# Two ways for each up product of an expert, for 384 or for 512 rows

## The chip, the cores and the metric

One core of one Trainium2 chip runs the whole program. The metric is the time of one execution on the device in microseconds (us). Three timed runs of the kernel before gave 1068.37, 1067.69 and 1065.72 us; their median is 1067.69 us.

## The reference: what is computed

Three stages follow one another, all in float32, on 3072 tokens of width 512.

```python
# 1  linear attention with decay, 4 sequences x 8 heads x 768 steps x 64
state = gamma * state + outer(k_t, v_t);  y_t = scale * q_t @ state
# 2  a dense gated layer, 512 -> 1536 -> 512
x = ((x @ w_a) * (x @ w_b)) @ w_out
# 3  eight experts, each token goes to the one with its largest logit
e_idx = argmax(x @ w_gate)                       # 3072 tokens, 8 experts
for e in range(8):
    h  = maximum(x[e_idx == e] @ w1[e], 0)       # up:   512 -> 1024
    ye = h @ w2[e]                               # down: 1024 -> 512
    out[e_idx == e] = gate_w * eom * ye
```

How many tokens an expert gets is known only on the chip, after the logits. The mean is 384.

## The kernel before, in words

The change lies in the third stage. `BASE, CAP = 384, 512` (L33): every expert is computed for 384 gathered rows, and a fourth tile of 128 rows only where the expert has more than 384 tokens. `n_e` is the count of an expert, held in a register of every engine. What is above 512 rows goes to a loop at the end (`overflow`, L676).

Matmuls are made in float32 precision out of three: `mm3` (L104 to 107) multiplies high and low halves of both operands, so each product of a 128x128 weight tile costs three matmuls, one per line. `up(p, f, d, c0, n)` (L626) makes the up product of feature tile `f` (there are `NF2` = 8 of 128 features) for `n` rows from `c0`: 4 weight tiles x 3 = 12 matmuls into one PSUM bank. `up2` (L632) does so into bank `ph[f % 2]`. `relu` (L639) turns that bank into the pair of halves `hs[f]`: one ScalarE instruction for the high half (L636), one VectorE instruction for the low half (L637). `down2` (L644) multiplies `hs[f]` with the second weight matrix, three matmuls of 512 columns for each tile of 128 rows, and adds them up in the banks `accs[t]` over all `f`. `finish` (L651) scales a finished bank and sends it to the output by an indirect DMA of POOL. While an expert runs, the weights of the next one are loaded by the SP queue (`load_raw`, L421) and split into halves (`split_part`, L668, ScalarE and VectorE), its rows are gathered by POOL (`gather`, L607) and turned by TensorE (`turn`, L615).

`expert` (L695 to 754) writes out the order by hand; every engine issues its instructions in the order of the program text. For each `f` TensorE makes `up2(f)` for 384 rows, then what `rest(f)` holds, then `down2(f - 1)`. `rest` (L707) is the part under a condition: `with tc.If(n_e > BASE)` (L714) makes the up product of the fourth tile (12 matmuls of 128 columns into the bank `px`), its relu (`hx`), and the down product of the fourth tile one step behind (three matmuls into `accs[3]`). It is called for `f` = 0 to 8, so an expert has nine such blocks; expert 0 has none, since it always has 512 rows, 256 of them done ahead. There is no `Else`. All five engines branch at each block, whether they have work in it or not. An engine that skips a block adds to its semaphore what the block would have added, so that later waits hold on either way; that addition waits until the engine's own earlier work is counted. At the end of an expert `up2(0)` of the next one is issued (L754), for 384 rows.

Of the kernel before, what the change touches and what calls it, by code (L numbers as in the profile page):

```python
# [7 lines left out]
F32 = mybir.dt.float32  # L8
F32R = mybir.dt.float32r
# [10 lines left out]
E, FF2 = 8, 1024  # L20
# [8 lines left out]
NF2 = FF2 // 128  # L29
# [3 lines left out]
BASE, CAP = 384, 512  # L33
LEAD = 256
# [19 lines left out]
def attention_moe_moe2(ctx: ExitStack, tc: tile.TileContext, a: dict, out: bass.AP):  # L54
# [4 lines left out]
    p2 = ctx.enter_context(tc.tile_pool(name="p2", bufs=2))  # L59
    ps1 = ctx.enter_context(tc.tile_pool(name="ps1", bufs=1, space=bass.MemoryType.PSUM))  # L60
    psg = ctx.enter_context(tc.tile_pool(name="psg", bufs=2, space=bass.MemoryType.PSUM))
# [6 lines left out]
    def lp(n):  # L68
        if not late:
            for _ in narrowing:  # L70
                pass
            early.close()
            for k in (1, 2, 3, 5):
                late[k] = ctx.enter_context(tc.tile_pool(name=f"l{k}", bufs=k))
        return late[n]
# [7 lines left out]
    arena = cpool.tile([128, NF1, 2, 2, 512], F32R, name="arena")  # L83
# [16 lines left out]
    idx = cpool.tile([128, E, 4, 4], I32, name="idx")  # L100
# [3 lines left out]
    def mm3(outp, wh, wl, rh, rl, start, stop):  # L104
        pe.matmul(outp, lhsT=wh, rhs=rh, start=start, stop=False)  # L105
        pe.matmul(outp, lhsT=wh, rhs=rl, start=False, stop=False)  # L106
        pe.matmul(outp, lhsT=wl, rhs=rh, start=False, stop=stop)  # L107

    def f32(ap):
        return ap.bitcast(F32)  # L110
# [310 lines left out]
    def load_raw(key, src):  # L421
        t = lp(2).tile([128, 2, 512], F32, tag="wraw", name="wraw")
        sync.dma_start(t, src)
        rawq[key] = t
# [121 lines left out]
    accs = {}  # L546
# [40 lines left out]
    def load_idx0(j0):  # L587
        rows = tab_d[LEAD * (j0 // 2) : LEAD * (j0 // 2) + LEAD, :]
        sync.dma_start(idx[:, 0, j0 : j0 + 2], rows.rearrange("(j p) c -> p j c", j=2))
# [17 lines left out]
    def gather(e, jt, rows=T):  # L607
        fetch(idx[:, e, jt], (e, jt), rows)
# [3 lines left out]
    def xst(e):  # L612
        return turned if e % 2 else xs

    def turn(key, d, c0):  # L615
        t = gath.pop(key)
        pt = psg.tile([128, 4, 128], F32, tag="gen", name="pg")
        for k in range(KD):
            pe.transpose(pt[:, k], t[:, 128 * k : 128 * k + 128], ident)
        s = slice(c0, c0 + 128)  # L620
        act.copy(d[:, 0, :, s], pt)
        dve.tensor_tensor(d[:, 1, :, s], pt, f32(d[:, 0, :, s]), op=ALU.subtract)

    ph = {}

    def up(p, f, d, c0, n):  # L626
        cc = slice(c0, c0 + n)
        for k in range(KD):
            kk = slice(128 * k, 128 * k + 128)
            mm3(p[:, :n], arena[:, f, 0, 0, kk], arena[:, f, 0, 1, kk], d[:, 0, k, cc], d[:, 1, k, cc], k == 0, k == KD - 1)  # L630

    def up2(f, d, c0, n, which=None):  # L632
        up(ph[f % 2 if which is None else which], f, d, c0, n)

    def relu_to(h, p, n):
        act.activation(h[:, 0, :n], p[:, :n], AF.Relu)  # L636
        dve.scalar_tensor_tensor(h[:, 1, :n], p[:, :n], 0.0, f32(h[:, 0, :n]), op0=ALU.max, op1=ALU.subtract)  # L637

    def relu(f, n, which=None):  # L639
        h = p2.tile([128, 2, 512], F32R, tag="gs", name="hs")  # L640
        relu_to(h, ph[f % 2 if which is None else which], n)
        return h

    def down2(f, h, rows, a0=0, t0=0):  # L644
        for t, m in enumerate(rows, t0):
            if f == 0:
                accs[t] = ps1.tile([128, 512], F32, tag=f"acc{a0 + t}", name=f"acc{a0 + t}")
            tt = slice(128 * t, 128 * t + m)
            mm3(accs[t][:m], h[:, 0, tt], h[:, 1, tt], arena[:, f, 1, 0], arena[:, f, 1, 1], f == 0, f == NF2 - 1)

    def finish(ix, t, y, m=128):  # L651
        y, ix, acc = y[:m, t], ix[:m], accs[t][:m]
        if t % 2:
            dve.tensor_scalar(y, acc, ix[:, 2:3].bitcast(F32), None, op0=ALU.mult)
        else:
            act.activation(y, acc, AF.Copy, scale=ix[:, 2:3].bitcast(F32))  # L656
        st = pool.indirect_dma_start(  # L657
            out=out[:, :],
            out_offset=bass.IndirectOffsetOnAxis(ap=ix[:, 1:2], axis=0),
            in_=y,  # L660
            in_offset=None,
            bounds_check=T - 1,
            oob_is_err=False,
        )
        tc.declare_no_dep(st.ins, group="rows", reason="each token's row is in one slot")
        tc.add_to_no_dep_group("rows", st.ins)

    def split_part(key, f, part):  # L668
        t = rawq[key] if part == 0 else rawq.pop(key)
        act.copy(arena[:, f, part, 0], t[:, part])  # L670
        dve.tensor_tensor(arena[:, f, part, 1], t[:, part], f32(arena[:, f, part, 0]), op=ALU.subtract)  # L671

    def ytile():
        return p1.tile([128, 4, 512], F32, tag="xraw", name="y")
# [17 lines left out]
                        down2(f, relu(f, 128, 1), [128])  # L692
                    finish(it, 0, ytile())

    def expert(e, j0, n, n_e=None):  # L695


        rows = [min(128, n - t) for t in range(0, n, 128)]
        d = xst(e)
        nx = e + 1  # L700
        more = nx < E
        hs, hx = {}, {}
        y = ytile()
        if n_e is not None:
            accs[3] = ps1.tile([128, 512], F32, tag="acc3", name="acc3")

        def rest(f):  # L707

            if n_e is None:
                return  # L710
            px = psg.tile([128, 512], F32, tag="gen", name="px") if f < NF2 else None
            if f < NF2:
                hx[f] = lp(2).tile([128, 2, 128], F32R, tag="hx", name="hx")
            with tc.If(n_e > BASE):  # L714
                if f < NF2:
                    up(px, f, d, BASE, CAP - BASE)
                    relu_to(hx[f], px, CAP - BASE)
                if f > 0:
                    h = hx.pop(f - 1)
                    mm3(accs[3], h[:, 0], h[:, 1], arena[:, f - 1, 1, 0], arena[:, f - 1, 1, 1], f == 1, f == NF2)  # L720
                if f == NF2:
                    finish(idx[:, e, 3], 3, y)

        if more:
            load_raw(("ex", nx, 0), a["ex"][nx, 0])
            load_raw(("ex", nx, 1), a["ex"][nx, 1])
        hs[0] = relu(0, n)
        rest(0)
        for f in range(1, NF2 + 1):
            if f < NF2:  # L730
                up2(f, d, 0, n)
                hs[f] = relu(f, n)
            rest(f)
            if more:
                split_part(("ex", nx, f - 1), f - 1, 0)
            if more and f <= 4:
                gather(nx, f - 1)
            if more or f < NF2 - 1:
                down2(f - 1, hs.pop(f - 1), rows)
            if more and f < NF2:  # L740
                split_part(("ex", nx, f - 1), f - 1, 1)
                if f + 1 < NF2:
                    load_raw(("ex", nx, f + 1), a["ex"][nx, f + 1])
            if more and 3 <= f <= 6:
                turn((nx, f - 3), xst(nx), 128 * (f - 3))
        if not more:
            tc.mark_branch_hint_location("over", "LikelyTaken")
        for t, m in enumerate(rows):
            for f in hs:
                down2(f, hs[f], [m], 0, t)  # L750
            finish(idx[:, e, j0 + t], t, y, m)
        if more:
            split_part(("ex", nx, NF2 - 1), NF2 - 1, 1)
            up2(0, xst(nx), 0, BASE)  # L754


    with tc.manual_schedule():
# [45 lines left out]
        for j, blk in enumerate(BLOCKS):  # L803
            n = 256 * len(blk)
            ntile = n // 128
            last = j == len(BLOCKS) - 1
            att = attention_steps(j + 1) if not last else []
            if last:
                first = lambda: (load_idx0(0), gather(0, 0, T - 256), gather(0, 1, T - 256))
# [69 lines left out]
        hs = {}  # L879
# [8 lines left out]
        n_e = []  # L888
# [17 lines left out]
        y = ytile()  # L906
        for t in range(2):
            finish(idx[:, 0, t], t, y)
        up2(0, xs, 0, LEAD)

        expert(0, 2, CAP - LEAD)
        for e in range(1, E):
            expert(e, 0, BASE, n_e[e])
        with tc.If(n_e[E] > CAP, preferred_fallthrough_block=True, label="over"):
            overflow()

# [69 lines left out]
```

## Time and profile before

| | |
|---|---|
| median of three runs | 1067.69 us |
| the profiled execution, its own time | 1067.26 us |
| its span, from the first to the last instruction | 1065.0 us |
| TensorE matmuls, busy | 1028.6 us (97%) |
| VectorE, ScalarE, POOL, busy | 615.7, 390.2, 278.6 us |
| mean granted TensorE clock | 0.986 of full speed |

The profile is of one execution. PE is TensorE's matmuls, PEld its weight loads, DVE is VectorE, ACT is ScalarE, SP issues most DMAs. The letter q behind an engine (PEldq, ACTq) means its sequencer, which handles branches and semaphores. Matmuls are pipelined: the duration of one contains its latency, and the distance between two starts is what one costs in a row of them. In the timeline a line has the start and the duration in us, the engine, the line of the kernel, the operation, output and inputs, the shape, and in brackets how long the engine sat idle before it and what ended that.

### The profile page before, as it was taken

The numbers are of one execution on the slowest core, as the hardware profiler recorded it, in microseconds if no ns is written. First come the engines' busy times: TensorE is split into PE (matmuls) and PEld (weight loads), VectorE is DVE, ScalarE is ACT, GpSimd is POOL, SyncE is SP. The second block draws the span as 40 slices with busy tenths as digits, with TensorE's granted clock in tenths as the row PEclk, the third lists the DMA queues.
The fourth block names the chain that finished last, engine by engine and source line by source line (L and its number), as shares of the span: only waits on it lengthen the run. The fifth ranks groups of instructions, "written<-read, shape, count | busy, mean of one in ns | idle before, by whom it ended". The sixth has DMA issues, their size and how long they took to land. (4 is left out here: it accounts for less than half of the span.)

```text
span 1065.0 us, 20296 instructions
## 1 busy us (share of the span) xinstructions
PE 1028.6 (97%) x7893; PEld 862.4 (81%) x7894; DVE 615.7 (58%) x1399; ACT 390.2 (37%) x791; POOL 278.6 (26%) x241
## 2 busy tenths in 40 slices
PE   6899999999999999999999999999999999999997
PEld 4687778888888788878888889898888899988876
DVE  5798887665675567655765763643644444445431
ACT  3466662223222332223222334442544433334331
POOL 1456442113121411231124243423202203030211
PEclk7799999999999999999999999999999999999999
DMA  8666645222532243224222423523644424243410
GB/s 319 215 220 226 204 151 171 90 80 62 179 118 80 60 149 124 96 61 158 80 67 63 159 71 110 149 90 94 224 137 167 167 79 158 91 160 122 164 65 27
DMA packets 51674, 138.61 MB, mean 130 GB/s; under 512 B 10973, under 2 KB 11229, under 8 KB 51552
## 3 DMA queue, kind: packets, MB, share of 16 engines
q1 hardware_dynamic: 43920, 117.16, 33.0%
q0 software_dynamic: 6928, 19.46, 5.8%
q8 instruction: 69, 1.13, 0.4%
q10 hardware_dynamic: 720, 0.57, 0.2%
q14 instruction: 37, 0.30, 0.1%
HBM read 121.37 MB, written 16.96 MB: 130 GB/s over the span
## 5 line engine op out<-in xcount | busy, mean ns | idle before, releaser
L105 PE MATMUL p<-xs,arena 128*128 128x512 f32 (+1 forms) x672 | 249.2, 371 | 8.1 <-DVE z L220 4.3
L107 PE MATMUL p<-xs,arena 128*128 128x512 f32 (+1 forms) x672 | 243.3, 362 | 0.6 <-POOL arena L458 0.6
L106 PE MATMUL p<-xs,arena 128*128 128x512 f32 (+1 forms) x672 | 243.1, 362 | 0.0
L515 POOL TENSOR_TENSOR wos<-wo,wos 128x512 fp32r<-128x512 f32 x72 | 99.3, 1380 | 281.2 <-ACT wos L514 275.9
L105 PEld LDWEIGHTS p<-xs,arena 128*128 128x128 f32 x672 | 127.7, 190 | 31.4 <-issue 9.1
L107 PEld LDWEIGHTS p<-xs,arena 128*128 128x128 f32 x672 | 127.7, 190 | 20.8 <-POOL arena L458 1.0
L106 PEld LDWEIGHTS p<-xs,arena 128*128 128x128 f32 x672 | 127.9, 190 | 18.9
L542 ACT CAST gs<-g_sb 128x512 fp32r<-128x512 f32 (+1 forms) x84 | 47.0, 559 | 213.5 <-DVE g_sb L540 213.5
L340 DVE SCALAR_TENSOR_TENSOR junkd<-x,wcol 128x512 bf16<-128x512 f32 x144 | 121.9, 847 | 3.6
L671 DVE TENSOR_TENSOR arena<-wraw,arena 128x512 fp32r<-128x512 f32 x112 | 77.5, 692 | 78.8 <-ACT arena L670 77.5
L105 PE MATMUL acc<-wos,gs 128*128 128x512 f32 x288 | 115.0, 399 | 0.0
L107 PE MATMUL acc<-wos,gs 128*128 128x512 f32 x288 | 113.2, 393 | 0.0
L106 PE MATMUL acc<-wos,gs 128*128 128x512 f32 x288 | 112.4, 390 | 0.0
L637 DVE SCALAR_TENSOR_TENSOR hs<-ph,hs 128x384 fp32r<-128x384 f32 (+1 forms) x72 | 38.0, 527 | 103.6 <-ACTq L714 64.9
L540 DVE TENSOR_TENSOR g_sb<-p,a_sb 128x512 f32<-128x512 f32 (+1 forms) x84 | 51.3, 610 | 79.2 <-PE p L107 70.0
L657 POOL DMA_INDIRECT out<-y,idx x27 | 27.7, 1025 | 263.1 <-ACT y L656 173.2
L670 ACT CAST arena<-wraw 128x512 fp32r<-128x512 f32 x112 | 68.7, 619 | 71.1 <-PE acc L107 65.6
L105 PE MATMUL acc<-arena,hs 128*128 128x512 f32 x200 | 82.6, 413 | 6.9 <-PEq L714 1.4
L543 DVE TENSOR_TENSOR gs<-g_sb,gs 128x512 fp32r<-128x512 f32 (+1 forms) x84 | 52.1, 621 | 52.5 <-ACT gs L542 52.5
L106 PE MATMUL acc<-arena,hs 128*128 128x512 f32 x200 | 79.1, 396 | 0.0
L107 PE MATMUL acc<-arena,hs 128*128 128x512 f32 x200 | 78.9, 394 | 0.0
L636 ACT ACTIVATE hs<-ph 128x384 fp32r<-128x384 f32 (+1 forms) x72 | 33.6, 467 | 117.1 <-PE ph L107 115.6
(167 smaller groups left out, 1803.5 us busy)
## 6 DMA issues: line engine op xcount, KB each, us to landing
wraw<-in_ex SPq DMA_DIRECT2D x64, 512.0 KB, 3.3
wo<-wo_d SPq DMA_DIRECT2D x72, 256.0 KB, 2.6
wide<-in_w_ab SPq DMA_DIRECT2D x24, 512.0 KB, 4.0
qk<-in_qk SPq DMA_DIRECT2D x23, 512.0 KB, 4.3
vk<-in_vk SPq DMA_DIRECT2D x23, 512.0 KB, 5.4
wcol<-in_wgt SPq DMA_DIRECT2D x20, 512.0 KB, 5.1
wide<-in_w_out SPq DMA_DIRECT2D x12, 512.0 KB, 4.2
x_d<-x SPq DMA_DIRECT2D x24, 256.0 KB, 2.1
```

The lines of the kernel that those rows point to most:

```text
L105: pe.matmul(outp, lhsT=wh, rhs=rh, start=start, stop=False)
L106: pe.matmul(outp, lhsT=wh, rhs=rl, start=False, stop=False)
L107: pe.matmul(outp, lhsT=wl, rhs=rh, start=False, stop=stop)
L340: dve.scalar_tensor_tensor(junk, x2t[i], 1.0, wc[:, e], op0=ALU.mult, op1=ALU.mult, accum_out=st["lg"][:, e0 + e : e0 + e + 1])
L515: pool.tensor_tensor(w[:, 1], t, f32(w[:, 0]), op=ALU.subtract)
L540: dve.tensor_tensor(g[:, :n], pb[:, :n], ta[:, :n], op=ALU.mult)
L542: act.copy(gs[:, 0, :n], g[:, :n])
L543: dve.tensor_tensor(gs[:, 1, :n], g[:, :n], f32(gs[:, 0, :n]), op=ALU.subtract)
L636: act.activation(h[:, 0, :n], p[:, :n], AF.Relu)
L637: dve.scalar_tensor_tensor(h[:, 1, :n], p[:, :n], 0.0, f32(h[:, 0, :n]), op0=ALU.max, op1=ALU.subtract)
L670: act.copy(arena[:, f, part, 0], t[:, part])
L671: dve.tensor_tensor(arena[:, f, part, 1], t[:, part], f32(arena[:, f, part, 0]), op=ALU.subtract)
```

## The change

The part under a condition is no longer a block beside the up product: the up product itself has two ways. `first(f)` opens the condition before `up2(f)`. Where the expert has more than 384 tokens it makes the three down matmuls of the fourth tile of the step before (`rest(f - 1)`), then `up2(f)` for 512 rows and one relu for 512; in the `Else` it makes `up2(f)` and the relu for 384 rows. `px` and `hx` are gone, the fourth tile is part of `hs[f]`. `last` does the same for the end: `rest(7)`, the down product of `f` = 7 and the output of the fourth tile in one way, the down product alone in the other. For the last expert only the first tile's products of `f` = 6 and 7 are in the two ways, the other tiles follow behind. The `up2(0)` that is issued for the next expert has two ways as well, by that expert's count (`after`). Expert 0 stays without a condition but for that last product.

```diff
-    def expert(e, j0, n, n_e=None):
+    def expert(e, j0, n, n_e, after):
...
-        hs, hx = {}, {}
+        hs = {}
...
         def rest(f):
-            if n_e is None:
-                return
-            px = psg.tile([128, 512], F32, tag="gen", name="px") if f < NF2 else None
-            if f < NF2:
-                hx[f] = lp(2).tile([128, 2, 128], F32R, tag="hx", name="hx")
-            with tc.If(n_e > BASE):
-                if f < NF2:
-                    up(px, f, d, BASE, CAP - BASE)
-                    relu_to(hx[f], px, CAP - BASE)
-                if f > 0:
-                    h = hx.pop(f - 1)
-                    mm3(accs[3], h[:, 0], h[:, 1], arena[:, f - 1, 1, 0], arena[:, f - 1, 1, 1], f == 1, f == NF2)
-                if f == NF2:
-                    finish(idx[:, e, 3], 3, y)
+            mm3(accs[3], hs[f][:, 0, BASE:], hs[f][:, 1, BASE:], arena[:, f, 1, 0], arena[:, f, 1, 1], f == 0, f == NF2 - 1)
+
+        def first(f):
+            hs[f] = p2.tile([128, 2, 512], F32R, tag="gs", name="hs")
+            if n_e is None:
+                if f:
+                    up2(f, d, 0, n)
+                return relu_to(hs[f], ph[f % 2], n)
+            with tc.If(n_e > BASE) as some:
+                if f:
+                    rest(f - 1)
+                    up2(f, d, 0, CAP)
+                relu_to(hs[f], ph[f % 2], CAP)
+            with some.Else():
+                if f:
+                    up2(f, d, 0, BASE)
+                relu_to(hs[f], ph[f % 2], BASE)
+
+        def seconds(some_rows, t0):
+            for f in (NF2 - 1,) if more else (NF2 - 2, NF2 - 1):
+                down2(f, hs[f], some_rows, 0, t0)
+
+        def last():
+            own = rows if more else rows[:1]
+            with tc.If(n_e > BASE) as some:
+                rest(NF2 - 1)
+                seconds(own, 0)
+                finish(idx[:, e, 3], 3, y)
+            with some.Else():
+                seconds(own, 0)
...
-        hs[0] = relu(0, n)
-        rest(0)
+        first(0)
         for f in range(1, NF2 + 1):
             if f < NF2:
-                up2(f, d, 0, n)
-                hs[f] = relu(f, n)
-            rest(f)
+                first(f)
...
-            if more or f < NF2 - 1:
+            if f == NF2 and n_e is not None:
+                last()
+            elif more or f < NF2 - 1:
                 down2(f - 1, hs.pop(f - 1), rows)
...
         for t, m in enumerate(rows):
-            for f in hs:
-                down2(f, hs[f], [m], 0, t)
+            if t and not more:
+                seconds([m], t)
             finish(idx[:, e, j0 + t], t, y, m)
         if more:
             split_part(("ex", nx, NF2 - 1), NF2 - 1, 1)
-            up2(0, xst(nx), 0, BASE)
+            with tc.If(after > BASE) as some:
+                up2(0, xst(nx), 0, CAP)
+            with some.Else():
+                up2(0, xst(nx), 0, BASE)
...
-        expert(0, 2, CAP - LEAD)
-        for e in range(1, E):
-            expert(e, 0, BASE, n_e[e])
+        for e in range(E):
+            expert(e, 0 if e else 2, BASE if e else CAP - LEAD, n_e[e] if e else None, n_e[e + 1])
```

## Rows read from the trace of the kernel before

**Rows 1.** The page's first part: busy time, share of the span, instructions.

```profile
PE 1028.6 (97%) x7893; PEld 862.4 (81%) x7894; DVE 615.7 (58%) x1399; ACT 390.2 (37%) x791; POOL 278.6 (26%) x241
```

**Rows 2.** Windows by expert (1, 3, 4): length, busy per engine, granted clock, DMA.

```profile
762.96:801.98 39.02, 37.67 (x186) 31.59 (x185) 19.59 (x32) 17.44 (x31) 6.57 (x7) 1.00 0.45 147
...
840.93:892.64 51.71, 51.71 (x306) 47.14 (x305) 21.45 (x39) 18.51 (x38) 7.02 (x8) 1.00 0.35 118
892.64:944.36 51.72, 51.72 (x305) 47.14 (x304) 21.49 (x40) 18.50 (x38) 8.03 (x9) 1.00 0.35 120
```

**Rows 3.** Tile px: count, ns min/median/max, first and last start.

```profile
L105 PE MATMUL px<-arena x32: 221/274/276, 843.0 to 886.7; 128*128 128x128 f32 x32
...
L105 PE MATMUL px<-xs,arena x32: 220/274/276, 894.7 to 938.4; 128*128 128x128 f32 x32
```

**Rows 4.** Timeline of TensorE in expert 3: where each run of matmuls begins.

```profile
848.49 0.40 PE L105 MATMUL acc<-arena,hs 128*128 128x512 f32 x1
...
850.59 0.33 PE L105 MATMUL ph<-arena 128*128 128x384 f32 x1
...
852.69 0.22 PE L105 MATMUL px<-arena 128*128 128x128 f32 x1
...
853.98 0.46 PE L105 MATMUL acc<-arena,hx 128*128 128x512 f32 x1
...
856.84 0.33 PE L105 MATMUL ph<-arena 128*128 128x384 f32 x1
```

**Rows 5.** Timeline of TensorE in the dense layer, twelve matmuls of 512 columns apart.

```profile
500.84 0.39 PE L105 MATMUL p<-xs,arena 128*128 128x512 f32 x1
...
503.59 0.39 PE L105 MATMUL p<-xs,arena 128*128 128x512 f32 x1
```

**Rows 6.** Timeline of TensorE around a skipped block of expert 1.

```profile
767.60 0.34 PE L107 MATMUL ph<-arena 128*128 128x384 f32 x1
...
768.09 0.47 PE L105 MATMUL acc<-arena,hs 128*128 128x512 f32 x1
...
768.39 0.39 PE L106 MATMUL acc<-arena,hs 128*128 128x512 f32 x1
...
768.62 0.39 PE L107 MATMUL acc<-arena,hs 128*128 128x512 f32 x1
```

**Rows 7.** Line L714 by sequencer: whole span, then 765.0 to 768.2, then 840.0 to 843.0.

```profile
L714 PEldq COMPARE_BRANCH  x81: 70/208/414, 761.8 to 1054.5; - x81
...
L714 PEldq EVENT_SEMAPHORE  x45: 51/51/51, 765.5 to 1054.8; - x45
...
L714 PEldq EVENT_SEMAPHORE  x2: 51/51/51, 765.5 to 768.0; - x2
...
L714 PEldq COMPARE_BRANCH  x1: 169/169/169, 842.0 to 842.0; - x1
```

**Rows 8.** Waits of the weight loads, 762 to 1061: total us, times, longest.

```profile
PEld acc L105 <- issue: 17.2, 38, 0.6
PEld ph L105 <- issue: 2.2, 5, 0.4
```

**Rows 9.** Timeline in expert 3: a relu at its start, then one of f = 1.

```profile
843.21 0.49 ACT L636 ACTIVATE hs<-ph 128x384 fp32r<-128x384 f32 x1 [0.89 <-PE ph L107]
...
846.27 0.33 PE L107 MATMUL ph<-arena 128*128 128x384 f32 x1
...
846.64 0.49 ACT L636 ACTIVATE hs<-ph 128x384 fp32r<-128x384 f32 x1 [1.82 <-PE ph L107]
...
847.16 0.56 DVE L637 SCALAR_TENSOR_TENSOR hs<-ph,hs 128x384 fp32r<-128x384 f32 x1 [2.02 <-ACT hs L636]
```

**Rows 10.** Groups by line and shape: instructions of 512 columns that read PSUM.

```profile
L535 ACT COPY a_sb<-p 128x512 f32<-128x512 f32 x60 | 35.0, 584 | 78.7 <-PE p L107 75.9 <-PE rp L319 2.8
...
L656 ACT ACTIVATE y<-acc,idx 128x512 f32<-128x512 f32 x16 | 11.0, 688 | 8.7 <-PE acc L107 8.6
...
L622 DVE TENSOR_TENSOR arena<-pg,arena 128x512 fp32r<-128x512 f32 x16 | 10.9, 683 | 0.0
```

## The prediction

> **What bounds the kernel now.** I read the page's first part, then windows by expert, then the tile that the change removes, then the timeline of TensorE, and last the line of the condition and the waits. The chain of waits says nothing here: it ends after one piece, the last output DMA. The first part says that TensorE is busy for 97% of the span, no other engine for more than 58% [rows 1]. So a change counts by what it takes from or adds to TensorE's row of matmuls, and by the holes in that row.
>
> The windows show two kinds of expert. Expert 1 takes 39.02 us, experts 3 and 4 take 51.71 and 51.72 us, at full granted clock in all three [rows 2]. The reader is to see that in the long ones the busy time of TensorE equals the window, while expert 1 has holes. The tile px says which experts enter the block: 32 matmuls of each line (4 weight tiles x 8 features) in one stretch from 843.0 and 32 in one from 894.7 [rows 3]. So only two of the seven experts with a condition have more than 384 tokens in this input, and five skip the block, nine times each. That agrees with the 45 semaphore additions on TensorE's sequencer [rows 7].
>
> **What a block costs where it is entered.** In expert 3 one whole step runs from 850.59 to 856.84: 6.25 us [rows 4]. Of it the up product for 384 rows takes 852.69 - 850.59 = 2.10, px 853.98 - 852.69 = 1.29, and twelve down matmuls (three of the fourth tile, nine of the others) 856.84 - 853.98 = 2.86. Nine down matmuls alone take 850.59 - 848.49 = 2.10, that is 0.233 each, so the fourth tile's three cost 0.76. A matmul of 384 columns costs 0.175, one of 128 columns 1.29 / 12 = 0.108: a third of the columns, over half of the time.
>
> **What a block costs where it is skipped.** Matmuls of 384 columns start 0.175 apart, but the last one before a skipped block and the first one behind it are 768.09 - 767.60 = 0.49 apart, and the next step is 0.30 in place of 0.233 [rows 6]: 0.32 + 0.07 = 0.39 us lost. The cause is not the branch: the one at 842.0 is handled 1.2 us before ScalarE gets the finished product at 843.21 [rows 7, 9], so TensorE's sequencer runs ahead. It is the semaphore addition, which stands at 768.0, when the last matmul (767.60 + 0.34) has just ended: it waits until TensorE has drained. The weight loads show the same holes, 38 in front of a down product and 5 in front of an up product [rows 8]; the 5 are the block of f = 0, one for each skipping expert. Check: by these prices an entering expert has 8 x (1.29 + 0.76) = 16.4 us of extra work and a skipping one 9 x 0.39 = 3.5 us of holes, 12.9 apart; the windows are 51.71 - 39.02 = 12.7 apart.
>
> **The change, part by part.**
>
> *The wide product, in the two entering experts.* Twelve matmuls of 384 and twelve of 128 become twelve of 512. The trace has this shape in the dense layer: twelve apart are 503.59 - 500.84 = 2.75 [rows 5]; at the pace of the down product it would be 12 x 0.233 = 2.80. A step then costs 2.75 to 2.80 for up and 12 x 0.233 = 2.80 for down, 5.55 to 5.60 in place of 6.25: 0.65 to 0.70 less. The step f = 0 has no down product: 2.10 + 1.29 = 3.39 becomes 2.75 to 2.80, 0.59 to 0.64 less. Per expert 7 x 0.68 + 0.62 = 5.4, for both 10.8 (10.3 to 11.1). TensorE is the bound in these windows, so this counts in full.
>
> *ScalarE and VectorE.* One relu of 512 in place of one of 384 and one of 128. Nothing waits on their total: in expert 3 they are busy for 18.5 and 21.5 of 51.7 us [rows 2]. I cost it at nothing; the cover is TensorE's row. Only the delay to the first reader counts, which is the next part.
>
> *rest(f - 1) moved to the head of the way.* It needs hs[f - 1]. From the last up matmul's start to ScalarE's start are 846.64 - 846.27 = 0.37, to be 0.43 with a matmul of 512; the high half then takes 0.58 to 0.69 (nearest rows of 512 columns out of PSUM), VectorE follows 0.03 after its end and takes 0.68 [rows 9, 10]. High half ready 1.0 to 1.1 after that start, low half 1.7 to 1.8. For f of 2 to 8 nine down matmuls stand between: rest would start 0.23 + 2.10 = 2.33 after it, its low half is read two matmuls later. 1.2 and 1.0 us to spare: no cost. For f = 1 nothing stands between, since up2(0) ends the expert before. TensorE then waits 1.1 - 0.23 = 0.87 for the high half, 0.2 more for the low half and loses 0.07 in the restart: I take 1.2 per entering expert (0 if the trace's order hid it, 1.8 if ScalarE came later; it sat idle for 0.89 before the relu at 843.21 [rows 9], so it comes in time). Two experts: +2.4.
>
> *The two ways and their joins.* A join must leave each semaphore at one value. TensorE counts 15 matmuls in the long way and 12 in the short one, so the short way has 3 to add, while ScalarE and VectorE count the same in both. No row of before shows a condition with an `Else`. Between nothing (the last matmul counts for them) and 0.39 per join (as in rows 6, with the addition at the end of the short way), I take 0.39, because the addition in the skipped block is exactly this case. Both ways are equal for TensorE at f = 0 (no matmuls) and at the new two-way up2(0). So a skipping expert pays 8 times (f = 1 to 7 and the end) and no longer 9: 5 x 0.39 = 2.0 less. The long way has nothing to add. Like ends keep the readers behind the join on the same count, which by these rows costs and saves no time.
>
> *Added branches.* 63 blocks become 70, on five sequencers. TensorE's branch takes 208 ns in the median [rows 7], but ahead of the work; after a join its sequencer has nine down matmuls, 2.1 us, to get ahead again. I cost it at nothing; without that cover it would be 0.2 x 70 = 14 us.
>
> The row says that a jump over the skipped block ends well ahead of the matmuls, and that no wait of a weight load for issue in this stage is over 0.6 us [rows 7, 8]. The Trainium skill, Runtime: NRT & Kernel Launch, section Instruction fetch mechanics, says that a taken branch whose target is not in the loaded window has to wait for a fetch of the target page. That speaks against the change, since now the entering experts jump too, over the `Else`; by the rows the jumps of this length have not paid it, and the sum goes by the rows. If they paid, it would be the second rival.
>
> **The sum.** -10.8 + 2.4 - 2.0 = -10.4 us. The profiled execution took 1067.26, which gives 1056.9; it lies 0.4 below the median of 1067.69, so I predict 1057 us. Its own range, from the bounds above: 1054 to 1060.
>
> **Rivals.**
> 1. *The joins cost nothing.* If the last matmul of the short way carries the three missing counts, the 40 waits that I keep vanish as well: 40 x 0.39 = 15.6 more, 1041.7 us. For it: both ways end in the same kind of instruction, so there is one to carry them. Against: the only additions in the trace are separate and wait for the drain. 25%.
> 2. *The long way pays at its end.* The entering experts had no hole at all; if the jump over the `Else` or its join costs them a hole, it is 9 places (f = 1 to 7, the end, up2(0)) x 2 x 0.39 = 7.0: 1064 us. Against: they jump today without one. 8%.
> 3. *Slower: rest at the head waits at every step.* If ScalarE or VectorE is held up behind a split of the next weights by more than the 1.0 us to spare, each of f = 2 to 8 costs the 1.2 us of f = 1: 7 x 2 x 1.2 = 16.8, so 1057 + 16.8 = 1074 us. It decides from about 2.3 us between the last up matmul and the high half. Against: the relu at 846.64 starts 0.04 after the product's end, in the middle of an entering expert [rows 9]. 8%.
>
> That the change doesn't do what it says would mean that the same two experts don't take the long way; the counts come from the same registers as before, so this has, with all else, 7%.
>
> **How the numbers follow.** Forecast 52%, rivals 25, 8 and 8%, the rest 7%. A measurement here can tell about 0.3%, 3.2 us. Faster by more than that: forecast, first rival, about half of the second and a little of the rest, 0.83. Within 0.3%: the other half of the second and about half of the rest, 0.08. Slower: the third and what is left, 0.09. The range of 1040 to 1064 takes in the first two cases and most of the second rival; outside are the third and the rest.
>
> **What would show it.** px gone, and 192 matmuls into ph of 512 columns, 0.23 apart. Windows of about 47.5 us for experts 3 and 4 (51.7 - 5.4 + 1.2) and 38.6 for a skipping one. 40 semaphore additions on TensorE's sequencer, each with a hole of 0.49 from start to start; none, and windows near 35.5, would be rival 1. One hole of about 1.1 us at f = 1 of experts 3 and 4, in front of the down product of the fourth tile; seven more in each would be rival 3. Holes at the end of the long way would be rival 2. The prediction is wrong if the windows of skipping experts move by more than 1 us, or those of the entering ones by less than 3.

## The result and the profile after

The changed kernel takes 1041.86 us (median of 4 runs, 1040.78 to 1043.57), the kernel before beside it 1067.68: ratio 0.9763, 95% interval 0.9744 to 0.9781, or 25.8 us less. The forecast was 10.7 us less. The time is that of the first rival, 1041.7. It lies outside the range that the prediction worked out from its bounds (1054 to 1060) and inside its wide one (1040 to 1064). The span fell from 1065.0 to 1040.1 us, at a granted clock of 0.986 in both.

The page's first part after the change answers to [rows 1]: TensorE stays the bound, with 192 matmuls and 20.0 us of busy time fewer.

```profile
PE 1008.6 (97%) x7701; PEld 845.2 (81%) x7702; DVE 610.4 (59%) x1383; ACT 383.9 (37%) x775; POOL 278.9 (27%) x241
```

The windows by expert of the changed kernel, experts 1 to 4 (columns as in [rows 2], to which they answer):

```profile
763.85:799.24 35.39, 35.39 (x186) 31.91 (x185) 18.86 (x31) 16.60 (x31) 6.81 (x6) 1.00 0.49 162
799.24:834.62 35.38, 35.38 (x186) 31.90 (x185) 18.24 (x30) 16.09 (x30) 6.88 (x7) 1.00 0.51 170
834.62:881.93 47.31, 46.57 (x210) 37.46 (x208) 19.74 (x32) 17.05 (x30) 6.88 (x7) 1.00 0.38 129
881.93:929.19 47.26, 46.52 (x209) 37.47 (x208) 19.59 (x32) 17.05 (x30) 8.24 (x8) 1.00 0.39 132
```

The entering experts 3 and 4 take 47.3 us (forecast 47.5). The skipping ones take 35.4 where 38.6 was forecast, and in them TensorE's busy time now equals the window (they moved by 3.6 us, and more than 1 us was the prediction's own sign of being wrong), while expert 1 had 1.35 us of idle time and several stretched starts before [rows 2, 6]. By the starts of the windows the 24.9 us of span are: experts 1 and 2 3.6 each, experts 3 and 4 4.4 and 4.5, the three skipping ones at the end with the output 9.7 (expert 5 began at 944.36 before and begins at 929.19), less 0.9 by which expert 1 began later in this execution. The forecast had 10.4 for the whole.

The timeline of TensorE in expert 1 of the changed kernel, at the place where [rows 6] had a hole:

```profile
767.86 0.34 PE L107 MATMUL ph<-arena 128*128 128x384 f32 x1
768.04 0.39 PE L105 MATMUL acc<-arena,hs 128*128 128x512 f32 x1
768.26 0.40 PE L106 MATMUL acc<-arena,hs 128*128 128x512 f32 x1
```

The last up matmul and the first down matmul start 0.18 us apart (0.49 before), the next step takes 0.22 (0.30 before). The join costs TensorE nothing. The sequencers' view of the three conditions (the product, the end, `up2(0)`) says why, beside [rows 7]:

```profile
L718 PEldq COMPARE_BRANCH  x72: 73/202/337, 762.5 to 1023.6; - x72
...
L735 PEldq COMPARE_BRANCH  x9: 73/202/212, 793.5 to 1025.9; - x9
...
L735 POOLq INC_SWDGE_SEM  x5: 470/610/665, 769.8 to 1003.3; - x5
L735 DVEq EVENT_SEMAPHORE  x5: 21/21/21, 799.3 to 1030.7; - x5
...
L771 PEldq COMPARE_BRANCH  x9: 70/202/320, 762.2 to 997.2; - x9
```

TensorE's branches are there, 90 in place of 81. Its 45 separate additions are gone. What is left is one addition of VectorE and one of POOL for the end of each skipping expert, where the short way has no instruction of theirs. The reading is that the last matmul of the `Else` also adds what the three missing ones would have added. The profile doesn't hold the amounts, so this is inferred, and the experiments test it.

The waits of the weight loads after the change, from 762 to the end (answers to [rows 8], whose 43 waits for issue are gone):

```profile
PEld acc L105 <- ACT hs L636: 2.7, 3, 1.2
PEld acc L107 <- DVE hs L637: 0.9, 2, 0.4
PEld acc L107 <- DVEq L735: 0.3, 1, 0.3
```

The largest is the wait at f = 1. The timeline of the changed kernel in expert 3 shows it:

```profile
837.13 0.39 PE L107 MATMUL ph<-arena 128*128 128x512 f32 x1
...
837.61 0.60 ACT L636 ACTIVATE hs<-ph 128x512 fp32r<-128x512 f32 x1 [1.60 <-issue]
838.23 0.69 DVE L637 SCALAR_TENSOR_TENSOR hs<-ph,hs 128x512 fp32r<-128x512 f32 x1 [1.47 <-ACT hs L636]
...
838.25 0.50 PE L105 MATMUL acc<-arena,hs 128*128 128x512 f32 x1 [0.74 <-ACT hs L636]
...
838.59 0.40 PE L106 MATMUL acc<-arena,hs 128*128 128x512 f32 x1
...
838.98 0.50 PE L107 MATMUL acc<-arena,hs 128*128 128x512 f32 x1
...
839.32 0.40 PE L105 MATMUL ph<-arena 128*128 128x512 f32 x1
```

From the last up matmul to the next product are 839.32 - 837.13 = 2.19 us. Four starts in a row would be 4 x 0.23 = 0.92, so the wait costs 1.27 (forecast 1.2). The product in two lengths, in the same expert:

```profile
842.07 0.39 PE L105 MATMUL acc<-arena,hs 128*128 128x512 f32 x1
...
844.86 0.39 PE L105 MATMUL ph<-arena 128*128 128x512 f32 x1
...
847.59 0.39 PE L105 MATMUL acc<-arena,hs 128*128 128x512 f32 x1
```

Down 2.79, up 2.73, the step 5.52 us (forecast 5.55 to 5.60; 6.25 before).

### The profile page after: what moved, and what is told of

Its sections match the earlier page's. It is cut to its first block, busy times and chain, and to the rows that moved or that the text cites. A ratio compares the mean times of both kernels' runs of the same rounds, so it can differ in the third digit from the quotient of the medians.

```text
span 1040.1 us, 19789 instructions
## 1 busy us (share of the span) xinstructions
PE 1008.6 (97%) x7701; PEld 845.2 (81%) x7702; DVE 610.4 (59%) x1383; ACT 383.9 (37%) x775; POOL 278.9 (27%) x241
## 5 line engine op out<-in xcount | busy, mean ns | idle before, releaser
L637 DVE SCALAR_TENSOR_TENSOR hs<-ph,hs 128x384 fp32r<-128x384 f32 (+2 forms) x72 | 40.1, 558 | 121.9 <-ACT hs L636 108.9
L671 DVE TENSOR_TENSOR arena<-wraw,arena 128x512 fp32r<-128x512 f32 x112 | 76.5, 692 | 48.4 <-ACT arena L670 38.6
L105 PE MATMUL acc<-arena,hs 128*128 128x512 f32 x216 | 86.7, 402 | 2.1 <-ACT hs L636 1.5
L107 PE MATMUL acc<-arena,hs 128*128 128x512 f32 x216 | 85.8, 397 | 0.0
L106 PE MATMUL acc<-arena,hs 128*128 128x512 f32 x216 | 85.4, 395 | 0.0
L636 ACT ACTIVATE hs<-ph 128x384 fp32r<-128x384 f32 (+2 forms) x72 | 35.4, 491 | 134.4 <-PE ph L107 88.9
```

## The experiments

All ratios are to the kernel before on the same chip, with the 95% interval. The theory: what saved the 15.6 us is that the short way holds an instruction of TensorE, which carries the missing counts. The rivals: where the branch stands, the `Else` as such, or the like ends.

**The changed kernel again (a1)**, as the measure for e1, e2 and e4, which ran on the same chip. e5, e6 and e9 ran on another, where the kernel before took 1071.87 in place of 1069.67 us, so their spans compare with a1's only to some 2 us; the ratios take this out.

> The changed kernel as it is, on the chip of the next three, as their measure. Theory (the last matmul of the short way carries the three missing counts, so all 45 holes of before are gone): -10.8 for the wide product, +2.4 for the wait at f = 1, -17.6 for 45 holes of 0.39: ratio 0.976. Rival (the holes went because the branch now stands ahead of the up product and is hidden): the same number here; the next runs tell them apart.

Measured: 1040.68 us, 0.9736 [0.9722, 0.9751], span 1040.3.

**One matmul of 8 columns in the skipped way of the kernel before (e1).** Into `px`, read by nobody.

```diff
-            px = psg.tile([128, 512], F32, tag="gen", name="px") if f < NF2 else None
+            px = psg.tile([128, 512], F32, tag="gen", name="px")
...
-            with tc.If(n_e > BASE):
+            with tc.If(n_e > BASE) as some:
...
+            with some.Else():
+                pe.matmul(px[:, :8], lhsT=tri[:, 0], rhs=gap, start=True, stop=True)
```

> The kernel before, with an Else of one matmul of 8 columns in each conditional block; its result is read by nobody. Blocks, their places and the narrow product stay. Theory: the small matmul carries the counts, TensorE does not drain; 45 x (0.39 - 0.11 for one more short matmul) = 12.6 us faster, about 1055 us, no separate semaphore addition on TensorE's sequencer and spacings of at most 0.30 around a skipped block. Rival (the place of the branch decides): no faster than before, 1068 to 1072 us.

Measured: 1056.23 us, 0.9876 [0.9860, 0.9892], beside 1069.67 for the kernel before on the same chip, that is 13.4 less. The timeline of TensorE, with the added matmul at L724, and the condition's line by sequencer:

```profile
772.57 0.34 PE L107 MATMUL ph<-arena 128*128 128x384 f32 x1
772.75 0.18 PE L724 MATMUL px<-gap,tri 128*128 128x8 bf16 x1
772.79 0.48 PE L105 MATMUL acc<-arena,hs 128*128 128x512 f32 x1
773.10 0.39 PE L106 MATMUL acc<-arena,hs 128*128 128x512 f32 x1
```

```profile
L714 PEldq COMPARE_BRANCH  x81: 70/202/339, 762.7 to 1040.8; - x81
...
L714 DVEq EVENT_SEMAPHORE  x45: 21/21/21, 767.5 to 1045.5; - x45
...
L714 ACTq EVENT_SEMAPHORE  x40: 17/17/17, 766.9 to 1044.6; - x40
```

The branches stand where they stood and the two ways end in different products, yet the additions of TensorE are gone and the start to start is 0.22 with the added matmul in it (0.04 of it its own); only the next step stays at 0.31. VectorE and ScalarE go on adding, and TensorE's row shows no cost of it. The branch's place as the cause falls.

**A ScalarE instruction in the skipped way instead (e5).** A copy of one column, read by nobody.

```diff
-            with tc.If(n_e > BASE):
+            with tc.If(n_e > BASE) as some:
...
+            with some.Else():
+                spot = p2.tile([128, 1], F32, tag="sf", name="spot")
+                act.copy(spot, iota8[:, 0:1])
```

> The kernel before, with an Else in each conditional block that holds one ScalarE copy of a single column, read by nobody, and nothing of TensorE. Theory (TensorE needs an instruction of its own in the short way): its 45 separate additions and holes stay, within 4 us of before. Rival (any Else, that is any second way, lets the join be merged): about 17 us faster than before, ratio 0.984.

Measured: 1070.89 us beside 1071.87, 0.9993 [0.9982, 1.0004]: no change. The condition's line by sequencer:

```profile
L714 PEldq EVENT_SEMAPHORE  x45: 51/51/51, 765.0 to 1058.5; - x45
...
L714 ACTq EVENT_SEMAPHORE  x2: 17/17/17, 891.9 to 943.6; - x2
```

ScalarE's additions fall from 40 to 2, TensorE's stay. The two stand at the end of experts 3 and 4, where now the long way is the one without a ScalarE instruction. So an `Else` frees only the engine that has an instruction in it, and of these two engines only TensorE's counts for the time. The profiled span, 1068.7, is 3.7 us longer than before's 1065.0; four of TensorE's 45 additions came late here and cost 4 us (last section), the other holes are as before.

**The fourth tile's down product under a condition of its own, ahead of the two-way product (e4)**, with no `Else`. The same is done ahead of the end.

```diff
+            if f:
+                with tc.If(n_e > BASE):
+                    rest(f - 1)
             with tc.If(n_e > BASE) as some:
                 if f:
-                    rest(f - 1)
                     up2(f, d, 0, CAP)
...
-            with tc.If(n_e > BASE) as some:
+            with tc.If(n_e > BASE):
                 rest(NF2 - 1)
+            with tc.If(n_e > BASE) as some:
                 seconds(own, 0)
```

> The changed kernel with the three down matmuls of the fourth tile in a block of their own without an Else, ahead of the two-way product and of the end. Theory: the skipping experts get 8 empty short ways each, 40 in all, each with a separate addition and a drain: 40 x 0.39 = 15.6 us slower than the changed kernel, 1057.5 us, which is what was predicted for it. Rival (the branch ahead of the up product hides the addition): within 2 us of the changed kernel.

Measured: 1080.37 us, 1.0110 [1.0092, 1.0127], span 1077.1: slower than before, 36.8 us of span over the changed kernel (a1). The sign was right, the size off by 2.4 times. The 40 additions are back (35 at the product, 5 at the end). The timeline of TensorE at one of them:

```profile
770.40 0.40 PE L107 MATMUL acc<-arena,hs 128*128 128x512 f32 x1
771.26 0.44 PE L105 MATMUL ph<-arena 128*128 128x384 f32 x1 [0.47 <-PEq L719]
771.54 0.33 PE L106 MATMUL ph<-arena 128*128 128x384 f32 x1
...
811.78 0.40 PE L107 MATMUL acc<-arena,hs 128*128 128x512 f32 x1
815.15 0.44 PE L105 MATMUL ph<-xs,arena 128*128 128x384 f32 x1 [2.97 <-PEq L719]
```

The sequencer in the same kernel, the skipped block's addition and the branch of the product behind it, 770.0 to 771.4, and the late addition:

```profile
L719 PEldq EVENT_SEMAPHORE  x1: 51/51/51, 770.8 to 770.8; - x1
...
L721 PEldq COMPARE_BRANCH  x1: 218/218/218, 771.0 to 771.0; - x1
...
L719 PEldq EVENT_SEMAPHORE  x1: 51/51/51, 814.7 to 814.7; - x1
```

The start to start is 0.86 us and the next step 0.28 in place of 0.175. Against 0.23 without a hole, that is 0.63 + 0.10 = 0.73, more than the 0.39 of [rows 6]. The addition waits for the drain (until the engine's earlier matmuls have ended), and the next branch stands right behind it, so it is handled while TensorE has nothing to do: 771.0, 218 ns, first matmul at 771.26. Thirty-eight such places at 0.7 to 0.9 (29.1) and two where the addition came late (3.37 us from start to start, as at 811.78, and 3.2; 6.3 with the next steps) make up 35.4 of the 36.8. Why those two additions came 2.5 us after the last matmul had ended (811.78 + 0.40, 814.7) is open. The second of them, in expert 6, cost once more: TensorE had nothing to do for 2.8 us, and a microsecond later the granted clock stood at its lower level (1.2 GHz) for some 3 us, where twelve matmuls took 1.6 us more than their full-clock steps. Behind the first, where TensorE had nothing to do for 3.0 us, the clock did not fall. The window 997.6 to 1000.8 (columns as in [rows 2], the last but two is the granted clock):

```profile
997.60:1000.80 3.20, 3.20 (x12) 2.91 (x11) 0.54 (x2) 1.00 (x2) 0.00 (x0) 0.52 0.49 164
```

**The same block with one matmul of 8 columns in an `Else` (e9)**, in both places, into `accs[3]`, read by nobody:

```diff
-                with tc.If(n_e > BASE):
+                with tc.If(n_e > BASE) as fourth:
                     rest(f - 1)
+                with fourth.Else():
+                    pe.matmul(accs[3][:, :8], lhsT=tri[:, 0], rhs=gap, start=True, stop=True)
```

> As the kernel with the block of its own ahead of the product and of the end, with an Else of one matmul of 8 columns that carries the counts; its result is read by nobody. Two branches now stand one behind the other, with no drain between. Theory: the branches run ahead of the work and cost nothing, 40 small matmuls cost 40 x 0.11 = 4.4: about 5 us slower than the changed kernel, ratio 0.978. Rival (two branches in a row cost by themselves): still over 15 us slower than the changed kernel, ratio over 0.988.

Measured: 1047.42 us, 0.9768 [0.9743, 0.9793], span 1045.3. The timeline of TensorE, with the added matmul at L722:

```profile
770.10 0.40 PE L107 MATMUL acc<-arena,hs 128*128 128x512 f32 x1
770.34 0.18 PE L722 MATMUL acc<-gap,tri 128*128 128x8 bf16 x1
770.37 0.42 PE L105 MATMUL ph<-arena 128*128 128x384 f32 x1
770.63 0.33 PE L106 MATMUL ph<-arena 128*128 128x384 f32 x1
```

Of the 36.8 us of span 5.0 are left (3.4 by the ratios), which is what the rows give: 0.27 from start to start in place of 0.23 and 0.26 for the next step in place of 0.175, 40 times 0.125. So two branches in a row cost nothing more as long as no drain stands before the second; without the matmul it was 0.86 from start to start. A theory that the second condition itself is dear falls.

**The block of its own behind the two-way product (e6)**, no `Else`, for f = 1 to 7:

```diff
             with tc.If(n_e > BASE) as some:
                 if f:
-                    rest(f - 1)
                     up2(f, d, 0, CAP)
...
+            if f:
+                with tc.If(n_e > BASE):
+                    rest(f - 1)
```

> The changed kernel with the fourth tile's three down matmuls in a block of their own without an Else, behind the two-way product for f = 1 to 7 (the end stays as in the changed kernel). Theory for the 38 us that this block cost ahead of the product, where 15.6 were expected: behind the drain stood at once the branch of the product, which could not run ahead; behind the product nine down matmuls follow, and a drain costs 0.39 again: 35 x 0.39 = 13.7, less the 2.4 of the wait at f = 1, 11.3 us slower than the changed kernel, ratio 0.984. Rival (each further block costs TensorE about 0.9 wherever it stands): 35 x 0.9 - 2.4 = 29 us slower than the changed kernel, ratio 1.001.

Measured: 1057.91 us, 0.9861 [0.9835, 0.9886], span 1056.2: 16 us of span over the changed kernel, 0.0125 by the ratios or 13.4 us. The timeline of TensorE at a late place and at an ordinary one, then the line of the condition:

```profile
773.53 0.48 PE L105 MATMUL acc<-arena,hs 128*128 128x512 f32 x1 [1.76 <-PEq L727]
...
777.63 0.34 PE L107 MATMUL ph<-arena 128*128 128x384 f32 x1
778.12 0.48 PE L105 MATMUL acc<-arena,hs 128*128 128x512 f32 x1
778.43 0.39 PE L106 MATMUL acc<-arena,hs 128*128 128x512 f32 x1
```

```profile
L727 PEldq EVENT_SEMAPHORE  x35: 51/51/51, 767.2 to 1045.5; - x35
```

At 27 of the 35 places the hole has the very shape of [rows 6], 0.49 and 0.31: nine down matmuls follow it and no branch, so 27 x 0.39 = 10.5. Four more have 0.50 to 0.99 from start to start and lose 2.2 in all. At four places, all at f = 2, the addition came late and the start to start is 1.79 to 2.11; they lose 7.4. Less the 2.4 of the wait at f = 1, which is gone here, that is 17.7. The span says 15.9, and expert 1 began 1.4 earlier in this execution than in a1 (its last up matmul of f = 1 starts at 766.83, in a1 at 768.23): 17.3. The ratios, over four runs, say 13.4. The price per join in the prediction was right; it is not paid where the short way has a matmul.

**The changed kernel with the fourth tile's down product behind the up product (e2)**, so that the two ways end unlike:

```diff
                 if f:
-                    rest(f - 1)
                     up2(f, d, 0, CAP)
                 relu_to(hs[f], ph[f % 2], CAP)
+                if f:
+                    rest(f - 1)
```

> The changed kernel with the three down matmuls of the fourth tile behind the 512 up product and its relu in place of ahead of them, so that the two ways end unlike on TensorE. Theory (only that the short way has a matmul to carry the counts matters, not how the ways end): no holes come back, and the wait at f = 1 of the two entering experts goes: 2.4 us faster than the changed kernel, about 1039.5 us. Rival (the ends must be alike): up to 35 holes of 0.39 come back in the five skipping experts, 13.7 us slower, about 1055 us.

Measured: 1039.03 us (1037.93 to 1039.83), 0.9715 [0.9701, 0.9730], beside 1040.68 (1040.55 to 1042.57) for the changed kernel on the same chip. The two intervals overlap by a hair, but all five of its runs lie below all five of the changed kernel; 1.65 us less by the medians, 2.9 by the spans. Expert 3's window:

```profile
834.00:880.20 46.20, 46.20 (x209) 37.60 (x208) 19.74 (x32) 17.04 (x30) 6.88 (x7) 1.00 0.40 132
```

46.20 in place of 47.31, TensorE's busy time equals the window: the wait at f = 1 is gone, and no hole came back at any join: the waits of the weight loads from 762 to the end name no issue.

```profile
PEld acc L105 <- ACT hs L636: 0.4, 1, 0.4
PEld acc L107 <- DVEq L736: 0.3, 1, 0.3
```

That both ways end in the same product is not what saves the time. This version is the fastest measured, though its lead over the changed kernel is no larger than the spread of one kernel's runs (about 2 us).

## Why the prediction was wrong in its size

The sign and the mechanism were right, and the mechanism was priced too low in one term. The failing step is *The two ways and their joins*: it bounded a join with an `Else` between nothing ("the last matmul counts for them") and 0.39 us, and took 0.39 "because the addition in the skipped block is exactly this case". It was not. In the skipped block TensorE had no instruction that could carry the counts, in the short way it has twelve. Measured: 0 in place of 40 x 0.39 = 15.6. With that one term at its other end the sum is 1056.9 - 15.6 = 1041.3; the changed kernel took 1041.86. The carrying instruction is shown to be the cause from both sides: given to the kernel before, it takes away 13.4 us (e1, the 8-column matmuls included); with the fourth tile's product in a block whose skipped way holds no matmul, the holes come back in the changed one (e4, e6); with a matmul there, they go (e9).

Point by point:

- *What a skipped block costs*, 0.39 by the addition and not by the branch: right. The e6 run repeats it at 27 places, and e1 takes 13.4 of 45 x 0.39 = 17.6 away; the added matmul gives back 0.04 and a next step longer by 0.08 at each place, 5.4 in all, so 12.2 by the rows.
- *The wide product*, 10.8 for both experts: right. The step is 5.52 in place of 6.25, and with the wait taken out an entering window went from 51.71 to 47.31 - 1.27 = 46.0, 5.7 less (forecast 5.4).
- *rest moved to the head*, 1.2 per expert: right, 1.27 in the timeline, and 1.1 less in the window when the move is undone (e2). At f of 2 to 8 there is no such wait, so the third rival falls.
- *ScalarE and VectorE* at nothing, but for that wait: right; the waits of the weight loads name them five times, 3.6 us in all, the three of ScalarE led by the one at f = 1.
- *Added branches* at nothing: right while they run ahead of the work. The e4 run shows the place where they don't: right behind a drain.
- *The long way pays at its end*: fell, the waits behind L735 and L771 come to one of 0.3 us, for VectorE's addition.

The argument for the first rival, that both ways end in the same kind of instruction, named the right place and asked for more than the runs need: the ways may end in different products and, in e1, in different shapes (e1, e2). What they share in every kernel without holes is that TensorE has some matmul in each; whether an instruction of another kind would do is not tested. The first rival had 25% and the forecast 52%. [rows 7] had the warning in it, had I asked what the additions stood in for: they were in a way that held no instruction at all, which is just what the change alters.

## What to carry to other kernels

Where a part of the program is skipped under a condition, look whether the engine that sets the time has an instruction in the way that skips. If it has none, each join can cost it a drain (0.39 us here); in this kernel one tiny matmul there, whose result nobody reads, took it away, and an instruction of ScalarE, which is not the bound, changed nothing. Don't let a second condition follow a drain at once, and put the matmuls whose input comes late behind work that doesn't need it.

## What was not expected of the hardware

A branch of TensorE, free when handled ahead of the work, costs about 0.35 us more than the drain alone when it follows one (0.73 in e4 beside 0.39 in e6).

A second thing stays open. In ten places of e4, e5 and e6 the addition came 0.7 to 2.6 us after the last matmul's end, in most others 0.04. All ten are at f = 2: of experts 1, 2, 5 and 6 in e5 and e6, of 2 and 6 in e4. ScalarE's relu, which reads what that matmul finished, is late by as much (e5, expert 1):

```profile
771.63 0.34 PE L107 MATMUL ph<-arena 128*128 128x384 f32 x1
...
773.07 0.49 ACT L636 ACTIVATE hs<-ph 128x384 fp32r<-128x384 f32 x1 [2.54 <-PE ph L107]
...
773.18 0.47 PE L105 MATMUL acc<-arena,hs 128*128 128x512 f32 x1 [1.21 <-PEq L714]
```

So not only TensorE's own sequencer saw the end of the product late. In e1 the relu at the same place is late as well, and there TensorE goes on without a hole, as the rows from 772.57 to 773.10 above show:

```profile
774.40 0.49 ACT L636 ACTIVATE hs<-ph 128x384 fp32r<-128x384 f32 x1 [2.32 <-PE px L724]
```

A drain thus makes TensorE wait for a count that it needn't wait for otherwise. All ten places fall while POOL gathers rows for the next expert: its queue (software_dynamic) fills 72% of the DMA engines' time from 811.1 to 812.9 in e6. Expert 7 gathers none and has no late place. But in the kernel before that queue fills 82% from 772.1 to 772.7, at f = 2 of expert 1, and the addition there is on time, so the load alone is not the cause. The Trainium skill, Runtime: NRT & Kernel Launch, section Instruction fetch mechanics, says that a taken branch to a place that isn't loaded waits for a fetch. The traces speak against that here: between the last matmul's end and the addition no packet of the instruction queues moves in nine of the ten places. What holds the count is open.
